# A fused attention-and-SoLU kernel whose written-out order of all steps is made anew

## The chip, the cores and the metric

The kernel runs on one core of a Trainium2 chip. The metric is the time of one execution on the device in microseconds (us); of several executions the median counts. A core has five engines with an instruction queue each: TensorE (PE, products; its weight loads are shown as PEld), VectorE (DVE), ScalarE (ACT), GpSimd (POOL) and SyncE (SP, which here issues all transfers between HBM and the core's memory). Each engine works through its own queue in order, and the engines wait for one another by semaphores.

## The reference

Two softmax reads between 512 tokens and 32 states, for 8 batches and 8 heads, give 544 rows per batch; those rows go through a feed-forward layer with the SoLU activation and a layer norm.

```python
# x: (8, 8, 512, 64)   state: (8, 8, 32, 64)   scale = 1/8
a      = softmax(scale * x @ state.T)        # over the 32 states
xread  = a @ state                           # 512 token rows
a2     = softmax(scale * state @ x.T)        # over the 512 tokens
sread  = a2 @ x                              # 32 state rows
rows   = concatenate([xread, sread], axis=2) # heads side by side: (8 * 544, 512)
h      = rows @ w_in                         # (4352, 1024)
solu   = h * softmax(h)
ln     = (solu - mean) / sqrt(var + 1e-6) * g_ln
out    = ln @ w_out                          # (4352, 512)
```

The activations are float32. The weights w_in and w_out arrive as 64-bit floats and are turned to float32 on the chip.

## The kernel before, in words

**Tiles.** The 4352 rows are 34 tiles of 128 rows: tiles 0 to 31 hold the token rows (tile t belongs to batch t // 4), tiles 32 and 33 hold the state rows of all batches. For the token rows the kernel never forms `xread`: it first multiplies state and w_in for each batch (a 256 x 1024 matrix per batch, "state_w_in"), and then h = a @ state_w_in.

**Steps.** The work is cut into named steps, each a Python generator; one step of the order runs a generator to its next `yield`. The names that the tables use are these:

- `l n`, `cl n`, `c n`: the load of one 512 KB piece of the weights (n 0 to 7 is w_in, row block n // 2 and column half n % 2; n 8 to 15 is w_out), and its conversion to float32: ScalarE takes the low words (L232), VectorE makes two bit operations (L243, L246), and VectorE or GpSimd the addition (L249).
- `Ls`, `G`: load and copy of the states; `LT b i`, `Ln b i`: loads of x in two layouts.
- `V b n`: column half n of state_w_in of batch b: 8 products on TensorE (L199; the trace has 16 records for them) and two evictions on ScalarE (L142). For batches 0 and 1 the result stays on the core (`swf`, its PSUM bank is called `swph`); for batches 2 to 7 it goes to HBM and is read back later (`Y`, `Z`, tiles `vt`, `kept`, `swf`; PSUM `swps`).
- `S b`: scores of batch b (TensorE, L199, tiles `sps`); `E b`: softmax over tokens; `A b` or, for batch 0 in two halves, `Ah 0 k`: softmax over states, which ends in `aT` (tiles 4b and 4b+1 of batch 0 need the first half, the other two the second); `R b`: the state rows (L421, L432).
- `P b j`, `wo n`, `wi c`: split of a float32 matrix into a high and a low part. A product of two split matrices is made as three products (high x high, low x high, high x low). Batch 0 and the output products of tiles 0 and 1 use plain float32 instead.
- `wg f`: rows of w_out scaled by -g (tile `wog`), on ScalarE (L267) or VectorE (L269).
- `H t`: h of tile t on TensorE (L473) into one of two pairs of PSUM banks; `C t`: maximum (L480), exponential (L483), product (L486), centring (L491 on ScalarE or L493 on VectorE), sum of squares (L498) and a root on GpSimd (L500 to L503); `D t`: a 32 x 32 block transpose on VectorE (L510) and a round trip through HBM (tiles `ub`, `ut`, `back`) that completes the transpose; `T t`: high part `uh` (L142 on ScalarE, L144 on VectorE) and low part `ul` (L147); `O t`: output products (L541 plain, L547 split), eviction (L554, L556) and store (L560).
- `K`: one product of two 128 x 128 identity tiles into a bank that nobody reads (L571, tile `warm`; the trace has two records for each).

**What sets the order.** The text `ORDER` lists all steps in one line of issue, `name*count` for several in a row. `issue` walks through it, so each engine's queue is that list with the other engines' instructions left out; nothing reorders it later. The string table `OPT` says which engine does a step with a choice (a, d, p for ScalarE, VectorE, GpSimd), and `PLACES` gives each tile its place in the core's memory or its PSUM bank. A tile that is put on a place waits until the last reader of the tile that was there is done. `T t` needs `D t`, which needs most of `C t`, which needs all of `H t`; TensorE fills that chain's time with products of other tiles, as the order says.

Of the kernel before, what the change touches and what calls it, by code (L numbers as in the profile page):

```python
# [39 lines left out]
V10 c7 K LT00 V20 c3*2 c5*2 cl7 K cl5 c5 LT01 S0 c7 cl12 Ah01 E0 Lg K*6 E0*5 Ah00 V10*2 Ah00*2 l1 cl1 Ah00 K Ah01*3 K  # L40
c1 K*2 Ls2 G2 K V30 l8 l10 K*2 V30 K*2 l9 l11 K V30 K*2 G2 V40*2 Lg LT10 K*2 Ah00 c8 V40 V50*2 c9 V50 c1*2 V01 Ah01
l13 Ah00 c8 Ah00 Lg c13 V51*2 V11 V51 E0*2 Lg cl8 V31 Ah00 l14 c13 Ah00 K l15 Y51 V31 c14*2 Lg V01*2 V31 cl14 c14 K c8
Ah01 cl13 V11 Ah01 K E0 c15 Ah01 V70 wg0 V70*2 Y30 H0*2 V11 P10 C0 Ah01 cl10 C0 P11 wg6 c10 V21 c10 V21*2 H1 Ln01 c12
Ln11 K*2 C0*2 c10 H1 Ln00 C1*2 V41 E0 C0 V71*2 V41*2 LT31 V71 H2*2 P11 Y31 c12 cl9 D0 C1 D0 C1 c15 V60*2 c11 V60 C1
c9*2 R0 wg1 D1 R0*3 C2 P10 R0 wo4 R0 LT11 S1 Z51 D1 H3 V61 H3 E1*4 D0 A1*2 wg4 c11 Y41 c13 wg5 cl11 c11 D1 C2*2 A1 Y40
A1 C3 T0 O0 wg2 wg3 T0 O0*4 C2 D2 C3 C0 Y50 O0*2 V61*2 LT41 T1 O1*4 T1 O1 cl15 c15 A1 wg7 E1 wo7 D2 C2 E1 C1 C3*2 D3
Y20 O0 A1*2 C2 O1*3 A1*3 Z31 D3 D2 H4 O1 LT21 C3 E1*2 A1 H5 wo5*2 wo4 H4*5 H5*2 D3 T3 H5*3 wo7 LT20 Y60 S2 E1 C4*2 C3
O3*2 C4 T3 O3 T3 O3 Ln10 Y61 O0*2 E2 T2 O3*2 E2 C4 wo6 E2*2 Z20 H6 O3*2 P31 T2 O2*2 C5 H6*2 Y71 D4*2 O1 O2*2 wo6 C5
O3*2 A2*2 C5 A2*2 C5 H7 D5 C5 A2 H6*3 O2 H7 T3 O3*2 O2 O3 T2 O2 T2 E1 C6 A2*2 P20*2 D4 C4*2 T4 O2*4 LT30 D5 H7*2 C6
O2*2 O4 R1*2 T4*2 O4 Y21 C6 O4*3 Z50 R1 A2 S3 D5 C6 E2 O4*2 A2*2 T4 Z21 D6*2 E3 O3 A3*2 A2 E2 Z30 E2 Y70 T5 O4 T5 O4  # L50
P21*2 H7*2 C7 H8*2 O5 D6 O5 O4 E2 E3 C7 O4*3 O5*2 T5 LT40 C7*2 T5 A3 T6 D7 O5*2 C6 H8*4 O5 D7 P31 O5*3 C8*2 E3 O2 E3*3
# [24 lines left out]
H32 C31*2 H32*2 C31 H32 D31 D30 D31 H32*3 wi2 H32*2 O28*3 H32 O28 H32*2 H33*2 O29*3 O25 O29*3 T30 T29 H33 O29 T30*2
O29*3 C32*3 D31 T31 C32 D32*2 C30 O29*2 H33*3 O29*2 O30 C30 T31 H33 T31*2 H33*5 O30*8 O31 C31 O31*5 C33*4 D33 C33 D32
T32*4 C33 O31*2 O28 O31*2 C31 O32*2 O31 O30 O31 T30 O30*3 D33*2 O30 T33 O32*6 O31*2 O33*4 T33 O32 C32 O32 O33 T33
O33*5 T33 O33 O32 C32 O32 O33*10 O32 O33 O32 O33*6
"""  # L80

# [6 lines left out]
    sm='0123103210321032103210321031023102',  # L88
# [567 lines left out]
```

## Time and profile before

| what | value |
|---|---|
| executions | 363.46, 363.64 and 366.76 us, median 363.64 us |
| the profiled execution | 366.5 us, span from first to last instruction 364.6 us |
| TensorE busy | 346.6 us (95% of the span) |
| VectorE busy | 282.6 us (77%) |
| ScalarE busy | 216.2 us (59%) |
| GpSimd busy | 190.2 us (52%) |
| DMA, main queue | 91.77 MB, 71.9% of 16 engines' span |
| granted TensorE clock | 1.000 |

A busy time is the time in which at least one instruction of that engine ran. In a list of groups, the columns are line, engine, operation, tiles, shapes and count, then busy time, mean duration of one in ns, and the idle time just before with what ended it. In a timeline the columns are start, duration from the first start to the last end of the merged run, engine, line, operation, tiles, shapes and count, and in brackets the idle time before it and what ended it. Products overlap in TensorE, so a row's duration is a little more than the distance to the next row's start.

### The profile page before, as it was taken

Reading aid. Unit: us, or ns where it says so; the run is one execution under the profiler, and the core shown is the slowest. Engines: PE = TensorE matmul, PEld = TensorE weight load, DVE = VectorE, ACT = ScalarE, POOL = GpSimd, SP = SyncE. Lnnn points to the kernel's source line nnn. Section 1 sums busy time; section 2 is a strip of 40 time slices with the busy share of each in tenths; the row PEclk is TensorE's granted clock in tenths of the full one; section 3 lists DMA queues with packets and bytes.
Section 4 is the critical chain, followed back from the end, with each engine's and each line's share of the span. In section 5 each row is a group of like instructions: output and inputs, shape, how many; then the busy total and the mean of one; then the engine's idle time right before and its main releaser. Section 6 shows DMA issues by size and latency. Waiting matters only on the chain.

```text
span 364.6 us, 6200 instructions
## 1 busy us (share of the span) xinstructions
PE 346.6 (95%) x2274; PEld 255.5 (70%) x2274; DVE 282.6 (77%) x393; ACT 216.2 (59%) x350; POOL 190.2 (52%) x245
## 2 busy tenths in 40 slices
PE   5399999999899999999999999999999999999996
PEld 4153333468677787868888677887888888888885
DVE  4679999979797878977988999889649767866500
ACT  3277998877657973848564765646367456324421
POOL 2131275646669564345959253538677743740280
PEclk9999999999999999999999999999999999999999
DMA  7995999999889999667796797585756145344442
GB/s 253 398 400 210 347 317 335 332 343 351 290 243 341 351 323 326 211 212 257 243 363 224 261 293 287 177 293 223 262 176 222 76 166 187 125 143 152 180 146 74
DMA packets 47086, 92.16 MB, mean 253 GB/s; under 512 B 4176, under 2 KB 25936, under 8 KB 47056
## 3 DMA queue, kind: packets, MB, share of 16 engines
q1 hardware_dynamic: 47056, 91.77, 71.9%
q8 instruction: 18, 0.29, 0.3%
q14 instruction: 12, 0.10, 0.1%
HBM read 54.53 MB, written 37.22 MB: 252 GB/s over the span
## 4 chain that ended last, share of the span: by engine, by line
PE 62%; DMA 14%; DVE 12%; issue 4%; ACT 4%; SPq 2%; POOL 1%; ACTq 0%; DVEq 0%; POOLq 0%
PE o L547 34%; PE h L473 20%; DMA back<-ut 6%; DMA ut<-ub 3%; DMA st<-stB_dram 3%; DMA kept<-vt 2%; PE swps L199 2%; PE swph L199 2%; DVE ub L510 2%; PE srps L421 2%; DVE sm L480 2%; PE sps L199 2%; DVE u L486 1%; ACT e L483 1%; DVE swl L147 1%
## 5 line engine op out<-in xcount | busy, mean ns | idle before, releaser
L147 POOL TENSOR_TENSOR ul<-back,uh 128x512 fp32r<-128x512 f32 x46 | 61.1, 1335 | 48.7 <-DVE uh L144 25.3
L547 PE MATMUL o<-wohi,uh 128*128 128x512 f32 (+1 forms) x264 | 70.6, 386 | 2.0 <-ACT uh L142 1.6
L547 PE MATMUL o<-wohi,ul 128*128 128x512 f32 (+1 forms) x264 | 71.3, 384 | 0.4 <-POOL ul L147 0.4
L547 PE MATMUL o<-wolo,uh 128*128 128x512 f32 (+1 forms) x264 | 71.3, 385 | 0.0
L483 ACT ACTIVATE e<-h,sm 128x1024 f32<-128x1024 f32 x34 | 37.9, 1114 | 39.3 <-DVE sm L480 36.0
L547 PEld LDWEIGHTS o<-wohi,uh 128*128 128x128 f32 x264 | 48.2, 188 | 13.7 <-ACT uh L142 2.4
L486 DVE SCALAR_TENSOR_TENSOR u<-h,e 128x1024 f32<-128x1024 f32 x34 | 41.4, 1218 | 20.7 <-ACT e L483 20.4
L547 PEld LDWEIGHTS o<-wohi,ul 128*128 128x128 f32 x264 | 48.7, 188 | 11.4 <-POOL ul L147 0.8
L547 PEld LDWEIGHTS o<-wolo,uh 128*128 128x128 f32 x264 | 48.3, 188 | 11.2 <-issue 1.7
L480 DVE TENSOR_REDUCE sm<-h 128x1 f32<-128x1024 f32 x34 | 41.2, 1213 | 14.0 <-PE h L473 8.2
L510 DVE STREAM_TRANSPOSE ub<-u 128x1024 f32<-128x1024 f32 x34 | 42.0, 1236 | 5.6 <-ACT u L491 5.0
L142 ACT ACTIVATE uh<-back 128x512 fp32r<-128x512 f32 (+1 forms) x46 | 28.2, 624 | 27.3 <-DMA back<-ut 27.3
L498 ACT ACTIVATE e<-u 128x1024 f32<-128x1024 f32 x34 | 35.8, 1052 | 5.6 <-DVE u L493 5.3
L554 ACT ACTIVATE osb<-o,sm 128x512 f32<-128x512 f32 (+1 forms) x29 | 19.2, 666 | 26.7 <-PE o L547 6.6
L473 PE MATMUL h<-swh,ath 128*128 128x512 f32 x112 | 35.0, 398 | 0.0
L473 PE MATMUL h<-swl,ath 128*128 128x512 f32 x112 | 34.5, 391 | 0.0
L473 PE MATMUL h<-swh,atl 128*128 128x512 f32 x112 | 34.4, 389 | 0.0
L491 ACT ACTIVATE u<-u,sm 128x1024 f32<-128x1024 f32 x20 | 23.0, 1150 | 13.5 <-DVE u L486 13.5
L147 POOL TENSOR_TENSOR swl<-swf,swh 128x1024 fp32r<-128x1024 f32 x11 | 26.4, 2399 | 2.9 <-ACT swh L142 1.7
L249 POOL TENSOR_TENSOR wf<-wf,r 128x512 uint32<-128x512 uint32 x9 | 11.8, 1310 | 27.7 <-DVE wf L246 11.4
L473 PEld LDWEIGHTS h<-swh,ath 128*128 128x128 f32 x112 | 20.6, 188 | 5.9 <-issue 1.7
L473 PEld LDWEIGHTS h<-swh,atl 128*128 128x128 f32 x112 | 21.0, 188 | 4.5
(87 smaller groups left out, 533.8 us busy)
## 6 DMA issues: line engine op xcount, KB each, us to landing
ut<-ub SPq DMA_DIRECT2D x34, 512.0 KB, 3.5
back<-ut SPq DMA_DIRECT2D x34, 512.0 KB, 4.5
out_dram<-osb SPq DMA_DIRECT2D x33, 256.0 KB, 3.8
xT<-xT_dram SPq DMA_DIRECT2D x16, 512.0 KB, 7.9
xn<-xn_dram SPq DMA_DIRECT2D x16, 512.0 KB, 6.4
kept<-vt SPq DMA_DIRECT2D x12, 512.0 KB, 6.6
swf<-kept SPq DMA_DIRECT2D x12, 512.0 KB, 6.3
raw<-w_in_dram SPq DMA_DIRECT2D x8, 512.0 KB, 8.5
```

The source lines that it names most:

```text
L142: nc.scalar.activation(out, src, AF.Copy)
L147: engine(k).tensor_tensor(out=out, in0=a, in1=hi.bitcast(F32), op=ALU.subtract)
L199: nc.tensor.matmul(banks[j][at:at + NS, :], state_of(b, head), moving(head // 2)[h * D:(h + 1) * D], start=True, stop=True)
L473: nc.tensor.matmul(ph[t][:, cols], left[l][:, p, tok], weights[:, cols], start=(p, l, r) == (0, 0, 0), stop=(p, l, r) == (parts - 1, *kind ...
L480: nc.vector.tensor_reduce(nm, ph[t], AX.X, ALU.max, negate=True)
L483: nc.scalar.activation(e, ph[t], AF.Exp, bias=nm, accum_out=z)
L486: nc.vector.scalar_tensor_tensor(out=u, in0=ph[t], scalar=1.0, in1=e, op0=ALU.mult, op1=ALU.mult, accum_out=su)
L491: nc.scalar.activation(u, u, AF.Identity, bias=su, scale=-float(DF))
L498: nc.scalar.activation(e, u, AF.Square, scale=float(DF) ** -0.5, accum_out=ss)
L510: nc.vector.transpose(ub, us[t][0])
L547: nc.tensor.matmul(po, ut[t][l][:, f, :], w[NP + f // 2][:, f % 2, cols], start=(hf, l, w is wohi, q) == (0, 0, True, 0), stop=(hf, l, q) ...
L554: nc.scalar.activation(o[:, cols], po, AF.Copy, scale=us[t][1])
```

## The change

The tables `ORDER`, `OPT` and `PLACES` are replaced; no function is changed, and the same products, conversions and transfers are made. One line is added to a table, so every line number after it is one higher. `ORDER` holds 27 `K` steps instead of 37. `OPT` moves some steps between engines: counted over the whole kernel, of the 64 low parts `ul` VectorE makes 25 instead of 18 and GpSimd 39 instead of 46; ScalarE makes 49 instead of 46 of the 68 high parts `uh`, 7 instead of 4 of the 8 scalings of w_out, and 30 instead of 27 full-width evictions of output tiles; VectorE makes 3 instead of 6 of those.

```diff
-OPT = dict(ph=2, k4=45, direct=[0, 1], hn=[0], vh=[0, 1], ah=[0], on=[0, 1], s2='pppp', add='ddddppdddppppppp',
-           whi='aaaa', wlo='ddpp', wg='daaaddda', woh='aaaa', wol='dppd', ev='aaaaaaaaaaaaaaaaaaaaaaaaaaaaaaaa',
+OPT = dict(ph=2, k4=45, direct=[0, 1], hn=[0], vh=[0, 1], ah=[0], on=[0, 1], s2='pppp', add='dpdpdddpppppppdd',
+           whi='daad', wlo='ddpd', wg='aadaaaaa', woh='adaa', wol='dppd', ev='aaaaaaaaaaaaaaaaaaaaaaaaaaaaaaaa',
...
 ORDER = """
-l0 cl0 l4 c0*3 c4 cl4 c4*2 l2 K c2 K*5 c2 l12 c12 K l6 c6*2 K*3 cl2 c2 cl6 c6 l3 c3 cl3 Ls0 G0*2 V00*3 l5 l7 c7 V20*2
+l0 c0*2 l2 c2 cl2 c2*2 Ls0 G0*2 K*4 cl0 c0 l6 cl6 l4 K*4 c6 c4 cl4 c4 c6 c4 l5 c6 c5*2 V30 cl5 K LT00 V30 c5 V30 l3
...
```

**SyncE, the start of the program.** The first loads are, before (`raw n` is the piece of weights of `l n`, `st` the states of four batches, `xT0` the x of batch 0):

```order
L220 DMA raw0_86<-w_in_dram 128x1024
L220 DMA raw4_90<-w_in_dram 128x1024
L220 DMA raw2_102<-w_in_dram 128x1024
L223 DMA raw12_114<-w_out_dram 128x1x1024
L220 DMA raw6_119<-w_in_dram 128x1024
L220 DMA raw3_133<-w_in_dram 128x1024
L176 DMA st0_138<-stB_dram 128x1024
L220 DMA raw5_156<-w_in_dram 128x1024
L220 DMA raw7_158<-w_in_dram 128x1024
L204 DMA xT0_0_187<-xT_dram 128x1024
L204 DMA xT0_1_200<-xT_dram 128x1024
```

and now:

```order
L221 DMA raw0_86<-w_in_dram 128x1024
L221 DMA raw2_91<-w_in_dram 128x1024
L177 DMA st0_99<-stB_dram 128x1024
L221 DMA raw6_112<-w_in_dram 128x1024
L221 DMA raw4_116<-w_in_dram 128x1024
L221 DMA raw5_131<-w_in_dram 128x1024
L205 DMA xT0_0_151<-xT_dram 128x1024
L221 DMA raw3_156<-w_in_dram 128x1024
L205 DMA xT0_1_160<-xT_dram 128x1024
L177 DMA st2_200<-stB_dram 128x1024
L221 DMA raw7_205<-w_in_dram 128x1024
```

The states move from seventh to third place, the second half of x of batch 0 from eleventh to ninth, and the piece of w_out that stood fourth to a later place. The four even pieces of w_in (0, 2, 4, 6), which the first column halves of state_w_in need, are complete at place five, as before.

**TensorE, the first product tiles.** Around the first two `H` steps there stands, before (`h0` is H of tile 0, `swps2` and `swps4` are `V 2 1` and `V 4 1`):

```order
L473 MATMUL h0_438<-swf0_0_143,aT0_0_388 128x512 x2
L473 MATMUL h0_438<-swf0_1_144,aT0_0_388 128x512 x2
L199 MATMUL swps2_0_1_460<-wf0_92,s2_0_140 32x512 x2
L199 MATMUL swps2_0_1_460<-wf1_106,s2_0_140 32x512 x2
L199 MATMUL swps2_1_1_461<-wf2_96,s2_0_140 32x512 x2
L199 MATMUL swps2_1_1_461<-wf3_121,s2_0_140 32x512 x2
L473 MATMUL h1_473<-swf0_0_143,aT0_0_388 128x512 x2
L571 MATMUL warm_104<-ident_74 128x128 x2
L473 MATMUL h1_473<-swf0_1_144,aT0_0_388 128x512 x2
```

and now (`sps1` is the scores of batch 1, `swps5` is `V 5 1`):

```order
L474 MATMUL h1_439<-swf0_0_258,aT0_0_349 128x512 x2
L474 MATMUL h1_439<-swf0_1_259,aT0_0_349 128x512 x2
L572 MATMUL warm_104<-ident_74 128x128
L200 MATMUL sps1_0_464<-xT1_0_374,s2_0_101 32x512 x4
L200 MATMUL sps1_1_465<-xT1_1_330,s2_0_101 32x512 x4
L474 MATMUL h0_486<-swf0_0_258,aT0_0_349 128x512 x2
L474 MATMUL h0_486<-swf0_1_259,aT0_0_349 128x512 x2
L572 MATMUL warm_104<-ident_74 128x128 x4
L200 MATMUL swps5_0_1_527<-wf0_88,s2_2_202 32x512 x2
```

Tile 1 goes ahead of tile 0, and the scores of batch 1 stand between them instead of after tile 2. Ahead of this place stand 14 of the 18 `V` and `S` steps that precede the first output product, where before there were 12. Of the 37 `K` steps before, 10 stood ahead of the first `V`, 25 from there to the first `H` and 2 after it; now 8, 8 and 11. All stand ahead of the first output product, before and now.

**ScalarE, ahead of the first output products.** The instructions around the first `uh` (high part, or plain copy for tiles 0 and 1) are, before:

```order
L142 ACTIVATE uh0_678<-back0_650 128x512
L267 ACTIVATE wog5_682<-wf5_458,ngT_82 128x512 x2
L142 ACTIVATE uh0_678<-back0_650 128x512
L491 ACTIVATE u2_669<-u2_669,sm2_605 128x1024
L483 ACTIVATE e3_693,sm3_676<-h3_629,sm3_676 128x1024
```

and now:

```order
L268 ACTIVATE wog4_633<-wf4_256,ngT_82 128x512
L143 ACTIVATE uh1_639<-back1_551 128x512
L233 ACTIVATE r11_661<-raw11_220 128x512
L268 ACTIVATE wog4_633<-wf4_256,ngT_82 128x512
L484 ACTIVATE e3_669,sm3_601<-h3_553,sm3_601 128x1024
L143 ACTIVATE uh1_639<-back1_551 128x512
L268 ACTIVATE wog5_556<-wf5_328,ngT_82 128x512
```

More scalings of w_out (`wog`) stand on ScalarE, close ahead of the products that read them, and the exponential of tile 3 stands between the two halves of the first `uh`.

More of the change, by code (lines that the diff above doesn't have):

```diff
@@ new lines @@
+T2 O3*2 E2 O3*2 Z21 O2 C5*2 O3*2 O2*3 A2*2 E2 Z61 T2 H6 O3*2 LT30 H6 D5*2 C7 R0 T4 C2 E2 R1*2 O2 H6*4 P20 C7 O2 E2
+O2*3 C7 R0 O0 C7 A2 C7 R1 Z41 O4*2 A2*2 R1 H9 O2 P21 O4*2 R1*2 P20 H9 T4 O4 T4 O4*3 C4 C6 A2 C6*2 T4 C6 D7 S3 E3 D6 C6
+O4*5 H9*2 P21 H9*2 C6 E3*4 D5 T5*2 E3 C5 H8 E3 H8 Y51 O5*3 H8 T5 H8*2 D7 D6 T5 O5 C9 O5*2 C9 E3 O5 C9 O5*5 O2 C9 D9 R0
+O5 Z31 P31 D7 D6 T7*2 H11*2 A3 T6 H8 C8 LT41 A3 H11 O7 A3 O7 C8 O7 C8 C9 D9 A3 C8 P31 T6 O7*3 O6*4 H10 P61 H10*2 O6*2
+T6 Z30 P30 O6 E2 T6 H10*3 P30 T7 O6 A3 O6*2 O4 O5 O6 D9 T9 Ln21 O6*2 D8 O7 LT40 C8 C9 A3*2 D8 O9 E2 Ln20 D8 C7 O9 O6
@@ new lines @@
+H11 O7*2 T7 O7*2 P61 O7 T9*2 C10 O9 H11 Ln31 O9*2 H11 O9*2 C10*3 E3 A3*2 D10 S4 A4 D10 O7 T8 Ln30 R2*3 O9*2 A3 C8
+C11*2 O8 T8 O8*5 H12 C10 C11*2 H12 A3 H12 H13 E3 H13 H12*2 A4 T8 O8*2 E4 T9 O8*2 T8 E4*2 C11 D10 Ln61 O8*2 A4*2 O7 O8
+H12 R3 T10 R3 Z40 R2 D11 E4*3 C12 H13 A4*3 D11 O10 C12 O10 LT50 T10 C12 O10*2 C10 R3 P40 O10 R2 H13 O9 H13*2 E4*2 LT51
+E4 D11 R2 O9*3 wi1 H14*3 O8 T10*2 O10*2 C13 C12 D12*2 C13*2 H14*3 S5 E5 P41 C13*2 R3*2 A4 R3 O10*4 T11 O11*2 O10*2
+T11*2 E4 O11*2 E5 O11*2 T11 D13 O11*2 D12 O9 A4 C14 D13 A5*3 H15*3 O11*3 A4*2 C14 H15 E5 C12 E5 C11 LT61 O11 T12*2
@@ new lines @@
+O12*4 C14 T12 O11 Ln41 O12*2 C14 H15 C14 T12 P40 D13 Ln40 H15 C15 LT60 D14 O12*3 P41 C15 H16 O12*3 O11 H16*2 T13*2 O10
+C15*2 T13 C14 H16*2 O13*3 H16 E5*2 H17*4 D15 Z50 D14 D15 Ln51 D14 R4*2 A5 C12 O12 S6 R4*2 C16 O13*2 D15 O13*5 C15 C16
+E6*2 R4 LT71 C16*3 E5*2 A5 T14 T13 O13*2 D16*2 H18*2 R4 A5 E5 A5 A6 C16 H17 O12 H18*2 C13 H18 O14 T14*3 D16 O13 H17
+T15 C17*2 T15*2 H18 O14 A6 O14*3 LT70 A6 O13 C17*3 O15*2 T15 O15*3 O14*2 Z51 Ln60 O14*4 O15*3 D17*2 P50*2 E6*2 E5
+O14*2 O15*2 H19 T16 H19*3 E6 O15 C18 E6 T16 E6 O16 P51 O16 C18 A5*2 Ln50 C15 O15*2 O16*2 T16 O16 H19 D17 H19 O16 C18
@@ new lines @@
+O26*2 O25*2 H29 O25 C26 O25*2 T25 C28*3 D28 C28 O26 wi0 O25*2 T27 O25*2 O27 O25 wi2 O27 C27 T27*2 H29*3 C29*4 O25
+H30*3 wi3 O27 H30*3 O26 O27*7 T27 O27*2 O26 D29 D28*2 H31 T28 wi2 O27 wi3 H31*3 O26 C30*2 D29 R7 X O26*2 H31 O26 T28
+C26 O28 H31 C30 O28 O26 X H32 O28 C30 D29 T29 C31*2 D30*2 O27 T28*2 H32*5 C31*3 O28*6 H32*2 D31 H33*2 C31 O26 O28*2
+H33 D31 H33 D31 H33*2 O28*2 H32*4 C32 T31*2 H33*4 T31 C32 H33 T31 H33 O31*13 C32*2 O29*2 D32 O29*2 D30 T29*2 D32*2 T29
+O29 T30*2 O29 C33 O29 O30*3 C33*2 O29*3 C33 D33*2 O28 O29*2 D33 O30 T32 O32 C29*2 O30 O32*3 T32 O32 T32*2 O32*2 O30
@@ L80 @@
+O32*2 T30*2 O30*2 O31 O30 O32 O29*2 T33*2 C32 T33*2 O30*2 O32 O30 C30*2 O30 O33 O30 O33*4 C33*2 O33*11 C32 O32*3
+O33*12
 """
 PLACES = dict(
[L84 to L87 removed]
@@ L94, in issue @@
+    sm='0123012301321032103210321031201323',
+    o='0100100101011010110101000101010101',
+    t='01231231231231231231231321321313213103231320213200302301123102113012330301231230132102301230',
+    h='01010101011101011010101010100101010101')
 def issue(nc, steps, order):
```

83 lines of the change are left out of this document (29 added, 54 removed).

## The prediction

> **What bounds the kernel now.** I read the page of the profile first, then a table by stage, then TensorE's timeline of the first 76 us. The page:
>
> ```profile
> span 364.6 us, 6200 instructions
> ...
> PE 346.6 (95%) x2274; PEld 255.5 (70%) x2274; DVE 282.6 (77%) x393; ACT 216.2 (59%) x350; POOL 190.2 (52%) x245
> ...
> PE 62%; DMA 14%; DVE 12%; issue 4%; ACT 4%; SPq 2%; POOL 1%; ACTq 0%; DVEq 0%; POOLq 0%
> ```
>
> TensorE is busy for 95% of the span and carries most of the chain that ended last. The table by stage cuts the span at the first useful product (14.64), the first product of an H step (36.97), the first output product (60.60) and the last product; its columns are the stretch, its length, and the busy time of TensorE, its weight loads, VectorE, ScalarE and GpSimd, the clock, the share of the DMA engines and GB/s:
>
> ```profile
> 0.00:14.64 14.64, 4.64 (x21) 4.35 (x21) 7.78 (x13) 4.63 (x6) 2.59 (x9) 1.00 0.86 307
> 14.64:36.97 22.33, 21.54 (x242) 10.05 (x243) 17.56 (x36) 14.53 (x29) 4.56 (x7) 1.00 0.85 323
> 36.97:60.60 23.63, 23.13 (x213) 8.96 (x206) 22.21 (x37) 21.24 (x37) 12.40 (x9) 1.00 0.96 321
> 60.60:361.10 300.50, 297.31 (x1809) 232.17 (x1807) 235.00 (x310) 175.37 (x279) 170.65 (x221) 1.00 0.70 242
> 361.10:364.60 3.50, 0.00 (x0) 0.00 (x0) 0.00 (x0) 0.43 (x1) 0.00 (x0) 1.00 0.21 75
> ```
>
> From 60.60 on, TensorE waits for only 300.50 - 297.31 = 3.2 us in 300. That stretch holds the same products after the change, so an order can save there 3.2 us at most. The rest is the opening: 60.6 us until the first output product, in which TensorE looks busy but in part with warm-up products. Its timeline there:
>
> ```profile
> 1.34 4.64 PE L571 MATMUL warm<-ident 128*128 128x128 f32 x20 [1.34 <-POOL ident masks.py:199]
> 14.64 2.62 PE L199 MATMUL swph<-wf,s 64*32 64x512 f32 x16 [8.66 <-POOL s L144]
> 16.34 2.62 PE L199 MATMUL swps<-wf,s 64*32 64x512 f32 x16
> ...
> 20.61 0.71 PE L571 MATMUL warm<-ident 128*128 128x128 f32 x4
> 21.25 1.09 PE L199 MATMUL sps<-xT,s 64*32 64x512 f32 x16
> 22.27 2.72 PE L571 MATMUL warm<-ident 128*128 128x128 f32 x22
> ...
> 31.45 1.09 PE L199 MATMUL swph<-wf,s 64*32 64x512 f32 x16 [0.79 <-DVE wf L249]
> ...
> 36.97 3.70 PE L473 MATMUL h<-swf,aT 128*128 128x512 f32 x8
> 40.60 1.09 PE L199 MATMUL swps<-wf,s 64*32 64x512 f32 x16
> ...
> 52.23 1.10 PE L421 MATMUL srps<-xn,e 128*32 128x64 f32 x64
> 53.83 0.45 PE L432 MATMUL srT<-ident,sr 128*64 128x64 f32 x8 [0.50 <-DVE sr L425]
> ...
> 60.59 13.90 PE L541 MATMUL o<-wog,uh 128*128 128x512 f32 x32
> ```
>
> TensorE waits 8.66 us for the copied states; the scores of batch 0 start at 21.25 and the first H at 36.97, 15.7 us later, with warm-up products in between. What feeds this opening is the load queue. The landings show in who waited for them: first, second, seventh and ninth transfer.
>
> ```profile
> 4.71 0.67 ACT L232 ACTIVATE r<-raw 128x512 uint32<-128x512 uint32 x1 [2.71 <-DMA raw<-w_in_dram]
> 5.95 0.67 ACT L232 ACTIVATE r<-raw 128x512 uint32<-128x512 uint32 x1 [0.57 <-DMA raw<-w_in_dram]
> ...
> 13.98 1.27 POOL L144 COPY s<-st 64x512 f32<-64x512 f32 x2 [4.79 <-DMA st<-stB_dram]
> ...
> 16.52 0.43 DVE L243 TENSOR_SCALAR wf<-raw 128x512 uint32<-128x512 uint32 x1 [2.80 <-DMA raw<-w_in_dram]
> ```
>
> All these transfers are 512 KB, and they land one after the other: (16.52 - 4.71) / 8 = 1.48 us apart on average. So a load's place in SyncE's queue gives its landing time, before and after.
>
> **The change part by part.**
>
> *States third.* They land near 8 us instead of 13.9, so the 8.66 us wait breaks up. But the first V step also needs the fourth and fifth transfer and their conversions on VectorE, so it ends near 15 instead of 17 us. What counts is the next step. The scores of batch 0 need both halves of x, now at places seven and nine instead of ten and eleven; the ninth landed at 16.5. The scores therefore start near 16.1 instead of 21.25.
>
> *From the scores to the first H.* Lower bound: the same 15.7 us as before, which puts the H step of tile 1 at 31.8. Upper bound: no gain, 36.97 (all that follows hangs on another engine). In between lies ScalarE, whose prices are:
>
> ```profile
> 23.76 0.69 ACT L355 ACTIVATE e2T<-sps,sc 128x512 f32<-128x512 f32 x1 [1.98 <-POOL sc L351]
> ...
> 29.45 0.63 ACT L386 ACTIVATE a<-a 128x512 f32<-128x512 f32 x1
> ...
> 49.21 2.05 ACT L142 ACTIVATE vt<-swps 128x512 f32<-128x512 f32 x4
> ```
>
> In the new order ScalarE's queue holds, from the first exponential of the scores to the last eviction that this H needs, 20 evictions at 0.51 (2.05 for four), 2 conversions at 0.67, and 2 + 2 exponentials, at 0.9 with their sums read and at 0.63: 10.2 + 1.3 + 1.8 + 1.3 = 14.6 us. The first exponential came 2.5 us after the scores began (23.76 - 21.25), so now near 18.6, and the H of tile 1 can start at 33.2 if ScalarE never waits. I take 33.7, near this row, since the wait for the states of the other batches (tenth place, near 18) lies beside it. That is 3.3 us earlier than 36.97, with two more V or S steps behind it.
>
> *From the first H to the first output product.* TensorE's queue has four H steps at 3.63 (40.60 - 36.97), three V, one S and the sums of R at 1.1, and 11 warm-up products, which are 22 records, 2.7 us as in the row at 22.27: 14.5 + 5.5 + 2.7 = 22.7 us. For waits I put the 0.79 + 0.50 = 1.3 us that TensorE had between 14.64 and 60.59. The first output product then comes at 33.7 + 22.7 + 1.3 = 57.7 instead of 60.6: **-2.9 us**. Bounds: no wait and H at 31.8 give 54.5 (-6.1); VectorE and ScalarE, both over 90% busy in this stretch before, give back all of it (0). The ten dropped warm-up products lie within this term, and are no gain of their own: where TensorE would stand idle anyway they cost nothing.
>
> *A store on SyncE.* The turned softmax of batch 0 now goes out at place 21, ahead of half of the x of batch 1, a piece of w_out and the loads of g, which all wait until VectorE has made it. Before, it stood behind all loads. The 20 loads ahead of it land until about 4.7 + 19 x 1.48 = 32.8, and VectorE makes it as its 32nd instruction, 13 ahead of the first half of `aT` that H needs at 33.7, and so some 6 us earlier: the load queue hides the wait. If it came 3 us after 32.8, g and the scalings of w_out would come as much later, and the first output product with them.
>
> *The turning of R of batch 0* (0.45 us) moves behind the first output product: **+0.45**. The part of it that was a wait is counted above.
>
> *Engines chosen anew.* Seven more low parts on VectorE and seven fewer on GpSimd, three more high parts and more scalings on ScalarE. From 60.6 on these engines are busy for 235, 171 and 175 of 300 us, so this load lies beside TensorE's work as long as each tile's chain ends in time. The waits of TensorE there were 3.2 us; I take 3.5 (**+0.3**), with none and three times as much as the ends.
>
> *The end.* The last tile is again tile 33 in two halves, and 3.5 us follow the last product as before: nothing.
>
> Sum: -2.9 + 0.45 + 0.3 = -2.15, about -2.2. The span becomes 362.4. The profiled execution took 366.5, 1.9 more than its span, so it becomes 364.3; it lies 2.9 above the median of the runs, and a stretch that is the same in each run moves all of them alike: 363.64 - 2.2 = **361.4 us**.
>
> **A rule weighed: the first products.** A warm-up record took 4.64 / 20 = 0.23 us at 1.34 and 2.72 / 22 = 0.12 at 22.27; the V steps at 14.64 and 16.34 lie 1.70 us apart, while such a group takes 1.09 from 21.25 on. TensorE thus needs its longer times for 4.3 to 6.6 us after useful work began (to 18.96 at least, to 21.25 at most). In the new order TensorE has 18.6 us with little work ahead of the scores, and fewer warm-up products. The Trainium skill, page "TensorE: Matmul & The Clock Gate", Part 1, says that the array runs at half rate after an idle window of about 3.4 us and at full rate after about as long of sustained work. By that rule the products behind the scores make themselves fast by about 20 us; the sum is unchanged unless gaps keep the array at half rate, which is a rival below. The trace agrees in kind; its 4.3 to 6.6 us are longer than the rule's 3.4.
>
> **The rivals.**
>
> *A, faster by over 1%.* TensorE does not wait at all until the first output product (-1.3), and half of its 3.2 us of waits later go (-1.9 against the 3.5 assumed): 361.4 - 3.2 = 358.2. For it: the steps are written so that every chain has cover. Against it: 3.2 us in 300 is already little, and a new order has its own misses.
>
> *B, no gain.* VectorE sets the pace. It was busy 22.21 of 23.63 us from the first H to the first output product, and the new order puts no less ahead of the first four block transposes on it: counted in its queue, 65, 76, 87 and 91 instructions instead of 63, 69, 84 and 87. If it idles in the opening as before (22.33 - 17.56 = 4.8 us), the first output product comes no earlier: 363.6.
>
> *C, slower: chains longer than their cover.* A tile's chain, from the last product of H to the first `uh`, costs by these rows (page, groups and DMA issues):
>
> ```profile
> L483 ACT ACTIVATE e<-h,sm 128x1024 f32<-128x1024 f32 x34 | 37.9, 1114 | 39.3 <-DVE sm L480 36.0
> ...
> L486 DVE SCALAR_TENSOR_TENSOR u<-h,e 128x1024 f32<-128x1024 f32 x34 | 41.4, 1218 | 20.7 <-ACT e L483 20.4
> ...
> L480 DVE TENSOR_REDUCE sm<-h 128x1 f32<-128x1024 f32 x34 | 41.2, 1213 | 14.0 <-PE h L473 8.2
> L510 DVE STREAM_TRANSPOSE ub<-u 128x1024 f32<-128x1024 f32 x34 | 42.0, 1236 | 5.6 <-ACT u L491 5.0
> L142 ACT ACTIVATE uh<-back 128x512 fp32r<-128x512 f32 (+1 forms) x46 | 28.2, 624 | 27.3 <-DMA back<-ut 27.3
> ...
> L491 ACT ACTIVATE u<-u,sm 128x1024 f32<-128x1024 f32 x20 | 23.0, 1150 | 13.5 <-DVE u L486 13.5
> ...
> ut<-ub SPq DMA_DIRECT2D x34, 512.0 KB, 3.5
> back<-ut SPq DMA_DIRECT2D x34, 512.0 KB, 4.5
> ```
>
> That is 1.21 + 1.11 + 1.22 + 1.15 + 1.24 + 3.5 + 4.5 + 0.62 = 14.5 us when nothing queues. The cover is the TensorE work that stands between in the order. From the chain that ended last, the price of a split product and what the two transfers cost where they met others:
>
> ```profile
> 85.91 4.12 DMA ut<-ub
> 90.08 6.94 DMA back<-ut
> ...
> 280.76 9.52 PE o L547 x42
> ```
>
> At 0.227 us a product (9.52 / 42) the smallest covers are now 17.4, 17.2 and 17.4 us for tiles 22, 24 and 27, and 15.9 and 15.4 for tiles 31 and 32; before they were 17.5, 16.2, 17.2 and 14.1 for tiles 24, 25, 28 and 33. With transfers of 11.1 us as above a chain takes 17.6, and any queueing on an engine is then a wait. It decides when the chains of 22, 24 and 27 take over about 20 us: three waits of 3 us make +9 on the forecast, 370.4. Against it: the covers before were no larger and TensorE hardly waited.
>
> *D, slower: TensorE keeps its longer times in the opening.* If gaps keep it at the 1.70 us of the first groups, the 13 V and S groups from 16.1 on take 1.70 each and the 7 warm-up products among them 0.46, together 25.3, and H starts at 41.4 instead of 33.7: +7.7, 369.1. It decides when such groups still take that long past about 30 us.
>
> **How the numbers follow.** The forecast has 0.43, A 0.25, B 0.15, C 0.12, D 0.05. A measurement of this kernel tells about 1% (3.6 us) from no change. Faster by over 1%, below 360.0: A and 0.05 of the forecast's own spread, 0.30. Slower by over 1%: C and D, 0.17. Within 1%: the rest, 0.53. The range leaves out the far part of A and most of C: 357.4 to 367.4.
>
> **What would show it.** In the changed profile: the scores of batch 0 near 16 us and the first H near 33.7; the first output product near 57.7; TensorE idle for about 3.5 us from there to the last product. B shows as an H step that is earlier but an output product that is not; C as rows of TensorE that wait for `uh` or `ul` beyond 4 us in all; D as V steps still 1.7 us apart after 25 us. The prediction is wrong if the opening is not shorter, or if the long stretch loses more than the opening gains.

## The result, and the profile after

The changed kernel takes 361.58 us (median of 14 runs, 359.52 to 363.06), the kernel before 364.87 (median of 14, 363.31 to 366.76): a ratio of 0.9906, 95% interval 0.9882 to 0.9930. The forecast was 361.4. The profiled execution took 360.81 us, its span is 358.7. The two profiled executions lie 5.7 us apart and the medians 3.3, because the one of before was among its longest and the one of after among its shorter ones; so the times below rest on medians, and the traces of several kernels are read beside each other where a place is named.

The page of the changed kernel:

```profile
span 358.7 us, 6148 instructions
PE 345.6 (96%) x2254; PEld 253.8 (71%) x2254; DVE 280.5 (78%) x392; ACT 218.5 (61%) x357; POOL 186.0 (52%) x239
PE 71%; DMA 13%; DVE 7%; issue 4%; ACT 2%; SPq 2%; POOL 1%; ACTq 0%; POOLq 0%; DVEq 0%
```

TensorE now carries 71% of the chain that ended last instead of 62%, VectorE 7% instead of 12%. The table by stage, cut at the first useful product, the first H, the first output product and the end of the last (columns as before: stretch, length, busy TensorE, weight loads, VectorE, ScalarE, GpSimd, clock, DMA share, GB/s):

```profile
0.00:9.24 9.24, 3.78 (x16) 3.49 (x16) 3.54 (x6) 2.51 (x3) 1.89 (x8) 1.00 0.75 250
9.24:34.94 25.70, 23.57 (x240) 7.12 (x241) 21.53 (x41) 17.71 (x35) 6.32 (x8) 1.00 1.01 381
34.94:58.96 24.02, 23.18 (x182) 10.63 (x183) 23.57 (x37) 21.22 (x37) 11.37 (x14) 1.00 0.74 247
58.96:355.10 296.14, 295.10 (x1818) 232.54 (x1816) 231.85 (x310) 176.88 (x284) 166.43 (x210) 1.00 0.72 249
355.10:358.70 3.60, 0.00 (x0) 0.00 (x0) 0.00 (x0) 0.19 (x1) 0.00 (x0) 1.00 0.31 109
```

The first output product comes at 58.96 instead of 60.60, 1.6 us earlier, where 2.9 were forecast. The long stretch is 296.1 instead of 300.5 us: 4.4 shorter, where it was forecast 0.75 longer. TensorE's timeline of the opening:

```profile
9.24 2.60 PE L200 MATMUL swps<-wf,s 64*32 64x512 f32 x8 [4.11 <-POOL s L145]
13.34 2.52 PE L200 MATMUL swps<-wf,s 64*32 64x512 f32 x8 [1.50 <-DVE wf L250]
...
16.51 2.11 PE L200 MATMUL sps<-xT,s 64*32 64x512 f32 x16
...
34.94 3.67 PE L474 MATMUL h<-swf,aT 128*128 128x512 f32 x8
...
47.39 1.98 PE L474 MATMUL h<-swf,aT 128*128 128x512 f32 x4 [0.84 <-DVE aT L398]
...
58.96 2.74 PE L542 MATMUL o<-wog,uh 128*128 128x512 f32 x6
```

The wait of 8.66 us for the states has become two, 4.11 and 1.50, and the scores start at 16.51 instead of 21.25. But the first H starts only 2.0 us earlier (34.94 against 36.97). What TensorE waited for behind the first output product, before and after (engine and line, whom it waited for: us in total, times, longest):

```profile
PE o L547 <- ACT uh L142: 1.6, 2, 1.0
PE srps L421 <- ACT osb L554: 0.6, 1, 0.6
PE o L547 <- POOL ul L147: 0.4, 1, 0.4
PE o L547 <- DVE uh L144: 0.4, 1, 0.4
```

```profile
PE sps L200 <- DMA xT<-xT_dram: 0.6, 1, 0.6
```

The list holds idle times over 0.15 us. Before, output products waited for `uh` and `ul`, the last steps of a tile's chain; after, no product of the whole stretch does.

### The profile page after: what moved, and what is told of

Same layout as the page of the kernel before. It is cut to its first block, busy times and chain, and to the rows that moved or that the text cites. A ratio compares the mean times of both kernels' runs of the same rounds, so it can differ in the third digit from the quotient of the medians.

```text
span 358.7 us, 6148 instructions
## 1 busy us (share of the span) xinstructions
PE 345.6 (96%) x2254; PEld 253.8 (71%) x2254; DVE 280.5 (78%) x392; ACT 218.5 (61%) x357; POOL 186.0 (52%) x239
## 4 chain that ended last, share of the span: by engine, by line
PE 71%; DMA 13%; DVE 7%; issue 4%; ACT 2%; SPq 2%; POOL 1%; ACTq 0%; POOLq 0%; DVEq 0%
PE o L548 40%; PE h L474 21%; PE o L542 3%; DMA back<-ut 2%; DMA xT<-xT_dram 2%; DMA raw<-w_in_dram 2%; PE sps L200 2%; DMA ut<-ub 2%; PE srps L422 2%; DVE sm L481 1%; DVE u L487 1%; DMA raw<-w_out_dram 1%; PE swps L200 1%; DMA xn<-xn_dram 1%; DMA out_dram<-osb 1%
## 5 line engine op out<-in xcount | busy, mean ns | idle before, releaser
L148 POOL TENSOR_TENSOR ul<-back,uh 128x512 fp32r<-128x512 f32 x39 | 52.7, 1360 | 69.0 <-DVE uh L145 29.8
L555 ACT ACTIVATE osb<-o,sm 128x512 f32<-128x512 f32 (+1 forms) x32 | 21.4, 672 | 42.6 <-PE o L548 20.8
L499 ACT ACTIVATE e<-u 128x1024 f32<-128x1024 f32 x34 | 35.8, 1054 | 12.3 <-DVE u L494 12.2
L143 ACT ACTIVATE uh<-back 128x512 fp32r<-128x512 f32 (+1 forms) x49 | 29.9, 622 | 17.3 <-DMA back<-ut 17.1
L474 PE MATMUL h<-swh,ath 128*128 128x512 f32 x112 | 36.5, 407 | 0.1
L148 POOL TENSOR_TENSOR swl<-swf,swh 128x1024 fp32r<-128x1024 f32 x12 | 31.0, 2584 | 3.7 <-issue 2.2
L200 PE MATMUL swps<-wf,s 64*32 64x512 f32 x192 | 19.4, 636 | 6.2 <-POOL s L145 4.1
L250 POOL TENSOR_TENSOR wf<-wf,r 128x512 uint32<-128x512 uint32 x9 | 12.9, 1438 | 22.7 <-DVE wf L247 17.2
```

The lines of the kernel that those rows point to most:

```text
L143: nc.scalar.activation(out, src, AF.Copy)
L148: engine(k).tensor_tensor(out=out, in0=a, in1=hi.bitcast(F32), op=ALU.subtract)
L200: nc.tensor.matmul(banks[j][at:at + NS, :], state_of(b, head), moving(head // 2)[h * D:(h + 1) * D], start=True, stop=True)
L474: nc.tensor.matmul(ph[t][:, cols], left[l][:, p, tok], weights[:, cols], start=(p, l, r) == (0, 0, 0), stop=(p, l, r) == (parts - 1, *kind ...
L499: nc.scalar.activation(e, u, AF.Square, scale=float(DF) ** -0.5, accum_out=ss)
L555: nc.scalar.activation(o[:, cols], po, AF.Copy, scale=us[t][1])
```

## The experiments

Two theories stood against each other at first: the prediction's (the opening gives the gain, the rest gives a little back), and one read from the two traces (the order behind the first output product gives most of it). The other parts (slots, engine strings, warm-up products, load places) were changed one at a time.

### Slots made anew, in both kernels

Only the strings of places change: each buffer takes the slot whose last reader stands furthest back in the order. The cut shows the string of the large buffers; those of the output rows (`o`) and of PSUM banks (`t`) are made anew as well.

```diff
 # kernel before
-    k4='0123456789ABCDEFGHIJKLMNOPQRSTUVWXYZabcdefghi0148BAFEKLQPNTOefcdMR6USgJVcTd...
+    k4='0123456789ABCDEFGHIJKLMNOPQRSTUVWXYZabcdefghi0148BAFEKLQPNTOcfdeRMU6gAJSPdT...
 # changed kernel
-    k4='0123456789ABCDEFGHIJKLMNOPQRSTUVWXYZabcdefghi204569DCEKPHLSFXgbQ6i4eM5GTPSg...
+    k4='0123456789ABCDEFGHIJKLMNOPQRSTUVWXYZabcdefghi240659CEDKPHLFSXQgb05ie6MGQTBR...
```

> The kernel before, order and engines untouched; only the slot strings (blocks, output rows, banks) are written anew, so that each buffer takes the slot whose last reader stands furthest back. In the kernel before 9 of 349 reused slots are written again less than 20 issued instructions after their last reader; with the new strings none. If slots written too soon make TensorE's later waits (3.2 us from the first output product on), they fall to about 1 us and the time to about 362.8 from 364.9. If not (my theory: the slots cost nothing), 364.9 +- 0.8.

> The changed kernel with slot strings made by the same rule (the slot whose last reader is furthest back), nothing else. It is the yardstick for the two mixed kernels, whose slots are made by that rule too. All theories: 361.6 +- 0.8; first output product near 59.0, waits of TensorE behind it near 1 us.

Measured: 365.93 us for the kernel before (1.0029 of its own time, 1.0007 to 1.0051) and 364.72 for the changed one (0.9985 of the kernel before, 0.9959 to 1.0010). Both expectations failed, the first narrowly: its range without an effect was 364.9 +- 0.8. Before did not get faster, and from its first output product on TensorE was idle for 3.0 us again (261.39 - 258.38), so these slots took no wait away; whether they put new ones in place of old ones was not tested. The changed kernel lost 3.1 us, nearly all of its gain. Its trace shows where: what VectorE waited for from 60 to 72 us, and what TensorE waited for behind the first output product:

```profile
DVE u L484 <- DMA kept<-vt: 3.7, 1, 3.7
```

```profile
PE h L471 <- DVE u L484: 1.9, 1, 1.9
PE sps L197 <- DMA xT<-xT_dram: 0.5, 1, 0.5
PE o L545 <- ACT osb L552: 0.4, 1, 0.4
```

The new `u` had been put into the slot of a `vt` whose store still stood in SyncE's queue. VectorE, which works in order, stood still for 3.7 us, the PSUM half that this step frees came free late, and TensorE waited 1.9 us. A third version makes only the string of the large buffers anew, and counts a buffer that a store reads last as taken for 100 more issued instructions:

> The changed kernel; only its block slots are made anew, by the rule of after_own_slots with one thing added: a buffer whose last reader is a store on SyncE's queue counts as free only 100 issued instructions later (there 9 of 51 such buffers were written again within 60 instructions, here none within 100). after_own_slots took 364.7 against 361.6, and VectorE waited there 3.74 us for the store of a `vt` whose slot the next `u` had taken. If such waits for stores are what foreign slots cost, the time comes back to 361.6 +- 0.8 and that wait is gone. If the slots cost in another way (banks, other readers), it stays near 364.7.

Measured: 361.58 us (0.9906 of the kernel before, 0.9870 to 0.9941), the changed kernel's own time, and TensorE's waits behind the first output product are one of 1.0 us, for x. So new slots for the large buffers cost nothing when those under a store are left alone, and the waits for a store, 1.9 us on TensorE, are the largest part of the 3.1 us. The rest is not separated: the third version has the `o` and `t` of the changed kernel, the second has its own.

### The two halves of the order, exchanged

The step list of one kernel up to its first output product, then the remaining steps in the order of the other, with slots by the first rule. Each step keeps the engine of the kernel that its place comes from, so order and engines go together here. Around the joint of the first (old steps are those from `Y51` on):

```diff
 c9 cl11 wg1 H2*2 C3 c11 K T1 K A1 K
-O1*3 wg3 S2 A1 C2*2 P10 Z20 C3*2 O1*2 C2 H7*2 ...
+Y51 Y30 Ln11 LT31 P11 C0 R0 P10 R0 wo4 R0 Z51 Y41 wg5 C3 C2 O1 wg3 O1*4 ...
```

> The order of the changed kernel up to its first output product, then all remaining steps in the order of the kernel before (tiles 0 and 1, and 2 and 3, change names there, since the new opening begins with tile 1; each step keeps the engines of the kernel its place comes from). If the prediction's split is right (the opening gives -2.9, the rest +0.3), the time is about 362.0 or below, against 364.9 before. If the gain is half from the order behind the first output product, as the two traces suggest (opening 60.6 to 59.0, -1.6; the rest about -1.7 of the 3.3 between the medians), about 363.3, with some 3 us of waits behind the first output product. If the opening gives nothing at the end, 364.9.

> The other way round: the order of the kernel before up to its first output product (with its 37 warm-up products), then the remaining steps in the changed order. If the prediction's split is right, about 365.2 (the old opening, and +0.3). If half of the gain is from the rest, about 363.2: first output product near 60.6, waits behind it near 1 us. If all of it is from the rest, 361.6.

Measured: 376.89 us (1.0342, 1.0296 to 1.0387) and 373.27 us (1.0225, 1.0185 to 1.0265): both far slower than either kernel, so the time as a whole decides nothing between the theories. TensorE's waits from 60 to 100 us, in the kernel with the new opening and in the one with the new rest:

```profile
PE o L531 <- ACT wog L257: 4.4, 1, 4.4
PE o L537 <- ACT uh L132: 3.1, 1, 3.1
```

```profile
PE sps L190 <- DMA xT<-xT_dram: 7.9, 1, 7.9
PE o L532 <- DVE wog L260: 1.7, 1, 1.7
```

At the joint the scalings of w_out and the loads of x of batch 2 are where the other half does not want them. Behind it the mixed kernels can be compared with their parents. All orders end with the same work: the last 1600 products hold 1032 split products of H and O in each (340 and 692, or 336 and 696, at the same price) and the same 48 half-width ones, scores, and products of R. Their stretch, in the kernel before and in the mixed kernel that ends in its order:

```profile
60.59:100.08 39.49, 38.51 (x210) 25.09 (x208) 34.62 (x44) 30.32 (x47) 23.88 (x34) 1.00 0.94 337
100.08:361.02 260.94, 258.81 (x1601) 207.09 (x1599) 200.39 (x269) 145.01 (x231) 146.78 (x188) 1.00 0.66 227
```

```profile
109.45:371.19 261.74, 258.76 (x1601) 206.89 (x1599) 204.06 (x269) 145.15 (x231) 146.90 (x190) 1.00 0.64 224
```

and in the changed kernel and the mixed kernel that ends in the new order:

```profile
58.96:98.39 39.43, 38.80 (x218) 25.44 (x217) 35.81 (x47) 30.52 (x48) 30.20 (x27) 1.00 0.96 346
98.39:354.78 256.39, 256.30 (x1601) 207.10 (x1599) 196.04 (x264) 146.04 (x236) 136.23 (x184) 1.00 0.68 234
```

```profile
111.23:368.58 257.35, 256.83 (x1601) 207.04 (x1599) 196.04 (x263) 146.69 (x236) 136.36 (x184) 1.00 0.66 230
```

The old order takes 260.9 and 261.7 us for them, the new one 256.4 and 257.4, whichever opening stands ahead. Read in the same way from the profiles of the other kernels that keep one order and set of engines:

| | first output product at | from it to the last 1600 products | the last 1600 products |
|---|---|---|---|
| kernel before | 60.6 | 39.5 | 260.9 |
| before_own_slots | 60.5 | 38.1 | 261.4 |
| before_27_warmups | 59.9 | 38.3 | 260.8 |
| changed kernel | 59.0 | 39.4 | 256.4 |
| after_own_slots | 59.9 | 41.7 | 257.1 |
| after_store_slots | 60.1 | 39.7 | 256.5 |
| after_states_sixth | 59.9 | 39.4 | 256.2 |

On the means of three and three, without after_own_slots, whose wait for a store falls into the second column, the opening gives 0.7 us, the next stretch takes 0.9 back, and the last 1600 products give 4.7 (with it 0.6, 1.4 and 4.5). The 0.7 is no more than single executions of one order differ by (59.9 to 60.6, 59.0 to 60.1); the 4.7 is far outside. The gain of the change sits in the last 1600 products, from about 100 us on. The means of three spans differ by 4.1 us, a little more than the medians of the two kernels (3.3).

### The engine strings, exchanged

The order and slots stay, the engine strings are those of the other kernel, with tiles 0 and 1, and 2 and 3, exchanged in the strings by tile. In the changed kernel, in short:

```diff
-add='dpdpdddpppppppdd', whi='daad', ath='aadaaaad', up='aaaddaaaaaadaaddadaaaadddaaaddaddd'
+add='ddddppdddppppppp', whi='aaaa', ath='aaadaaad', up='dadadaaaaaaadadaaaaaadaddadadadddd'
```

> The changed order, slots and places, with the engine strings of the kernel before (tiles 0 and 1, and 2 and 3, exchanged in them, since the new order exchanges their parts). Prediction's term for the engines: +0.3, so without them 361.3 (361 to 362). If the engines make the gain: 364.9. If engines, slots and order only fit as a set, as the slots have shown: slower than 363, with waits of TensorE behind the first output product above 2 us.

> The kernel before with the engine strings of the changed kernel (tiles 0 and 1, and 2 and 3, exchanged). Prediction's term: 365.1. If the engines make the gain: 361.6. If they only fit their own order: slower than 366.

Measured: 398.04 us (1.0889, 1.0831 to 1.0947) and 404.85 (1.1090, 1.1041 to 1.1138): 36 and 40 us more than the same order with its own engines. The largest of TensorE's waits in the changed order with the old engines, over the whole span:

```profile
PE swps L193 <- DVE wf L243: 8.6, 2, 4.5
PE o L541 <- DVE ul L141: 4.8, 4, 1.5
PE o L535 <- DVE z L385: 4.6, 1, 4.6
PE o L541 <- DVE uh L138: 3.5, 3, 2.1
```

The amount of work on each engine differs little between the strings (VectorE 241 of 322 us there, 232 of 296 in the changed kernel behind the first output product). That leaves the place of an instruction in an engine's queue: one that has to wait for an operand holds up all that stands behind it. This is how the waits are read here; the slots, which were written for the other engines, may have a part in them, and no run tells the two apart. A part of the loss is the clock: around some of these waits the granted clock fell to 0.50 (from 70.0 to 76.5 us, for one), and TensorE is busy for 306.0 us behind the first output product, where it is 295.1 in the changed kernel. Neither string is better as such.

### The warm-up products alone

Ten fewer in the kernel before, nothing else (two from the first group, eight from the middle):

```diff
-l2 K c2 K*5 c2 ... cl7 K cl5 c5 LT01 ... E0 Lg K*6 E0*5 ... cl1 Ah00 K Ah01*3
+l2 c2 K*4 c2 ... cl7 cl5 c5 LT01 ... E0 Lg E0*5 ... cl1 Ah00 Ah01*3
```

> The kernel before with 27 instead of 37 warm-up products, nothing else: two less of the ten ahead of the first V step and eight less of the 25 between it and the first H. My theory (they only fill what is idle): 364.8 +- 0.6, first output product at 60.6. If they cost TensorE its time, 10 x 0.24 = 2.4 us less: 362.4. If fewer of them let the clock down, later than 364.8, with V groups 1.70 us apart beyond 21 us.

Measured: 364.63 us, 0.9989 of the kernel before (0.9965 to 1.0014), first output product at 59.93. These ten only filled idle time; the other 27 were kept.

### The load places of the opening

The states back behind the fourth and fifth piece of w_in; and, apart from that, the two halves of x of batch 0 behind three more loads. Every buffer keeps its slot.

```diff
-l2 c2 cl2 c2*2 Ls0 G0*2 K*4 cl0 c0 l6 ... c4 l5 c6 c5*2 V30
+l2 c2 cl2 c2*2 K*4 cl0 c0 l6 ... c4 l5 Ls0 G0*2 c6 c5*2 V30
```

```diff
-cl5 K LT00 V30 c5 V30 l3 c3*2 LT01 S0 ... E0*2 Ls2 G2*2 l7 c7
+cl5 K l3 Ls2 l7 LT00 V30 c5 V30 c3*2 LT01 S0 ... E0*2 G2*2 c7
```

> The changed kernel with the load of the states and its two copies behind the fourth and fifth piece of w_in (sixth instead of third place); every buffer keeps its slot. The states then land near 12.2 instead of 8.0 us and their copies end near 14, but the pieces of w_in land one place (1.3 us) earlier. My theory (x, at places seven and nine, sets the scores): scores near 17, time 361.6 +- 0.8. If the states at place three make the gain of the opening: V and scores about 3 us later, and 1.5 to 3 us at the end.

> The changed kernel with the two halves of x of batch 0 at places ten and eleven, as before, instead of seven and nine (three loads go ahead of them; slots kept). Scores about 19.9 instead of 16.5 to 17.3. If the chain from the scores sets the opening, as the prediction says, H comes 2.7 us later and so does the end: 364.3. If VectorE's work sets it (rival B) and no more than part of the delay lands on VectorE: 361.6 to 362.6.

Measured: 361.27 us with the states sixth (0.9899 of the kernel before, 0.9873 to 0.9925), the same as the changed kernel. Its TensorE:

```profile
13.87 2.98 PE L197 MATMUL swps<-wf,s 64*32 64x512 f32 x16 [8.74 <-POOL s L142]
16.78 0.79 PE L569 MATMUL warm<-ident 128*128 128x128 f32 x2
17.50 1.62 PE L197 MATMUL sps<-xT,s 64*32 64x512 f32 x16
```

The wait of 8.7 us for the states is back, as long as in the kernel before, and costs nothing: with the states at place three TensorE waits twice instead, the second time for a converted piece of w_in, and in both kernels the scores follow straight behind these products and two warm-up records. With x later, 363.27 us (0.9944, 0.9926 to 0.9963): 1.7 more than the changed kernel, or 1.4 by the two ratios. The scores began at 17.27 and not near 19.9, but they stopped for the second half of x:

```profile
17.27 3.30 PE L197 MATMUL sps<-xT,s 64*32 64x512 f32 x16 [0.77 <-DMA xT<-xT_dram]
```

H came at 37.86 and the first output product at 60.80, 2.3 and 1.1 us later than in three kernels with x in its new places (the changed kernel, after_store_slots and after_states_sixth, on the mean 35.6 and 59.7): a part of the delay was taken up on the way. The last 1600 products took 257.1 there. With an opening as long as the old one, the kernel kept more than half of its gain.

### VectorE in the opening

Seven last additions of the conversions to VectorE; in the other kernel three to GpSimd:

```diff
-add='dpdpdddpppppppdd'
+add='dpdpdddddddddddd'   # after_adds_on_vector
+add='dpdpddpppppppppp'   # after_adds_on_gpsimd
```

> The changed kernel with seven last additions of the conversions (pieces 7 to 13) on VectorE instead of GpSimd: 7 x 0.67 = 4.7 us more on VectorE in the opening, 7 x 1.28 = 9 us less on GpSimd. VectorE had 0.4 us of idle time in the 24.0 us between the first H and the first output product. If VectorE sets the pace there, the first output product moves from 59.0 to 62 - 63.7 and the time to 364.6 - 366.3. If not: 361.6 +- 0.8.

> The opposite: the additions of pieces 6, 14 and 15 on GpSimd instead of VectorE, 3 x 0.67 = 2.0 us less on VectorE, 3 x 1.28 = 3.8 us more on GpSimd, which is idle for half of that time. If VectorE sets the pace: 359.6 to 360.6. If what the additions feed then comes later, since GpSimd takes twice as long for one: 361.6 or above.

Measured: 369.13 us (1.0106, 1.0087 to 1.0124) and 363.02 us (0.9933, 0.9916 to 0.9950). The first is slower than any theory had it: the first output product came at 67.0, some 7 us late, for 4.7 us of work. What TensorE waited for longest from 20 to 43 us there, and VectorE from 35 to 43:

```profile
PE swps L193 <- DVE wf L243: 4.1, 1, 4.1
```

```profile
DVE z L383 <- ACT a L380: 2.6, 1, 2.6
DVE wf L243 <- ACT r L226: 2.5, 1, 2.5
```

The additions need ScalarE's rounding, and VectorE, in order, waited for it: a place in a queue adds to the amount of work. And the wait of 4.1 us was followed by slow products: the granted clock was 0.50 from 35.6 to 38.9 us, and four records of a V group took 1.92 us, where 16 take 1.09 elsewhere. The second kernel takes 2.0 us of work off VectorE, and its first output product comes at 59.80, where the mean above has 59.7. So this relief did not shorten the opening, and later a product waited 1.2 us for a low part on GpSimd (`atl`). It does not free VectorE of blame: GpSimd takes 1.28 us for an addition, VectorE 0.67, so what the additions feed comes later as well, and the time is in the range that was expected for that case. Rival B's sum of work alone foretells neither run.

## Why the prediction was right in the sum and wrong in its parts

*The total.* 361.4 forecast, 361.58 measured. That they agree is luck. The change was forecast as -2.2 us and measured as -3.3 (364.87 to 361.58); the forecast counted from the median of three executions, 363.64, which lies 1.2 below the median of fourteen, and this made up for the difference. And -2.2 itself is a sum of two errors: the opening gave less than forecast, the rest gave where it was to take.

*States third, scores near 16.1.* Nearly right: 16.51, though the profiled execution is the earliest; in six other kernels with this opening or with the states sixth the scores start at 17.16 to 17.50. Right too that the states themselves count for nothing and the places of x do: the runs with states sixth and x tenth show it.

*From the scores to the first H: forecast 33.7, measured 34.94, in the variants with slots, states or three additions changed 35.8 to 36.0.* ScalarE's row was priced well: 14.6 us forecast from the first exponential to the last eviction that H needs, 14.99 measured (19.76 to 34.75), and 14.99 or 15.00 in those four variants too. That ScalarE alone is in charge is not shown: in that stretch it is busy for 13.83 us and VectorE for 13.59, and VectorE's `aT` ended at 34.79, the eviction at 34.75. The step that failed is the one ahead of it. The first exponential came 3.25 us behind the scores (3.2 to 3.5 in the variants) instead of 2.5, because the scores themselves were slow:

```profile
16.51 2.11 PE L200 MATMUL sps<-xT,s 64*32 64x512 f32 x16
17.16 1.17 PE L189 MATMUL sps<-xT,s 64*32 64x512 f32 x16
```

The first row is the changed kernel, the second new_opening, which has the same steps up to here. Where the scores took 1.17 us the exponential came 2.73 us behind their start. The 2.5 us were read from the kernel before, whose scores at 21.25 took 1.09; here they come while TensorE still takes its longer times. The prediction had weighed these longer times, up to about 20 us, and left the sum unchanged.

*From the first H to the first output product.* 24.0 forecast (22.7 + 1.3), 24.02 measured.

*The term of the opening.* -2.9 forecast; -1.6 between the two profiled executions, -0.7 between means of three, and on these means nothing is left of it where the last 1600 products begin (98.9 before, 99.2 after).

*The turning of R moved behind (+0.45).* It stands in the 0.9 us that the stretch up to the last 1600 products is longer.

*Engines chosen anew, waits behind the first output product (+0.3).* The failed step, and the larger one: about -4.7 in the last 1600 products. The waits of TensorE there fell from 2.1 us (260.94 - 258.81) to 0.1 (256.39 - 256.30), where they were thought to rise. And the bound that the prediction set, "an order can save there 3.2 us at most", did not hold, since 2.5 us more came out of TensorE's busy time itself, 258.8 against 256.3 us for the same products. Most of this goes with the waits all the same, as the starts of the products in the kernel before show:

```profile
201.12 1.78 PE L199 MATMUL sps<-xT,s 64*32 64x512 f32 x16
...
204.78 0.61 PE L473 MATMUL h<-swl,ath 128*128 128x512 f32 x2
205.24 0.61 PE L547 MATMUL o<-wohi,ul 128*128 128x512 f32 x2
206.25 1.20 PE L547 MATMUL o<-wohi,uh 128*128 128x512 f32 x4 [0.39 <-DVE uh L144]
```

From the start of a row of two products to the next start 0.46 us pass where nothing waits (204.78 to 205.24), and 1.01 where the next product waits for `uh` (205.24 to 206.25); the four behind it take 1.20 us, where four take 1.07 elsewhere. Since products overlap, the row shows 0.39 us of idle time for what cost about 0.7. Four such waits stand in that stretch, 2.1 us of idle time that cost about 3.0. And two of the five groups of scores stretch without any idle time over 0.15 us: 1.78 and 1.45 us, where one takes 1.09 in the changed kernel. TensorE is busy with these 80 records for 6.49 us before and for 5.45 after. Together that is some 4.0 of the 4.5 us; for the rest no place is named. So the step that failed is to take the idle time in the list of waits for all that an order can give. Slots hardly count here: with new ones the stretch took 261.4 and 257.1 us, where each kernel's own gave 260.9 and 256.4. How much is the order and how much the engines stays open, since no run has one without the other that does not wait in many new places.

*Slots.* The prediction gave them no term. In the changed kernel they are worth 3.1 us against a simple rule, most of it ahead of the last 1600 products.

*Warm-up products, no gain of their own; the store on SyncE hidden.* The first is shown by its run. For the second, VectorE's scaling of g ran at 43.69 without a wait for its load; the store was not moved in a run of its own.

*The end, 0.* From the last product's end to the end of the span 3.6 us before (364.6 - 361.02) and 3.9 after (358.7 - 354.78).

*The rivals.* A was right in its later half: the idle time of the long stretch fell from 3.2 to 1.0 us. In its first half it was wrong: TensorE still waited ahead of the first output product, 0.84 us for `aT` at 47.39. B put VectorE in charge from the first H to the first output product. VectorE was busy for 23.57 of the 24.02 us there, but B's sign, an earlier H without an earlier output product, did not show: on the means of three H came 0.8 us earlier and the output product 0.7. C did not happen: no product waited for `uh` or `ul`, with covers of 17.2 us and, near the end, 15.4. D did not happen: V groups of 1.09 us stand from 18.97 on. But the longer times that D is about are what delayed the first exponential.

## What to carry to other kernels

An engine that is 95% busy does not bound what a new order can gain by its idle time: a short wait costs more than the idle time that its row shows, so compare the same set of products in two traces, not only the waits between them. Where queues work in order, the order, the engine of each step and the slot of each buffer are one choice; parts taken from another solution cost 1 to 40 us here, so a planner has to write all three together, and a buffer that a queued store still reads is not free. What a shorter opening gives is not read at its own end: take the difference at a point where both orders have the same work left. And a forecast of a change should be checked against the measured change: here the total was right and the change was not.

## What the runs showed of the hardware

Two things were not expected. First, VectorE's scaling of `u` takes 0.75 us in ten of its 14 places and took 2.68 at 63.38, beside GpSimd's subtractions; its reductions and products beside the same ones kept their 1.19 to 1.21:

```profile
61.01 1.19 DVE L481 TENSOR_REDUCE sm<-h 128x1 f32<-128x1024 f32 x1
62.12 1.21 DVE L487 SCALAR_TENSOR_TENSOR u<-h,e 128x1024 f32<-128x1024 f32 x1
...
63.38 2.68 DVE L494 TENSOR_SCALAR u<-u,sm 128x1024 f32<-128x1024 f32 x1
```

```profile
63.16 2.36 POOL L148 TENSOR_TENSOR atl<-aT,ath 128x1024 fp32r<-128x1024 f32 x1
65.47 2.82 POOL L148 TENSOR_TENSOR swl<-swf,swh 128x1024 fp32r<-128x1024 f32 x1
```

The scaling ends 0.5 us behind the subtraction that began just before it. The Trainium skill, page "SBUF — State Buffer", section "SBUF: two separate sides", says that VectorE, in some of its modes, and GpSimd share a pair of ports as an exclusive lock, which the first holds for its whole instruction while the other is blocked; the trace agrees for this form. Which engine gets a scaling is thus not only a matter of its own queue.

Second, a granted clock of 1.00 does not always show what the first products cost. From the end of the warm-up products on, in the changed kernel and in the one with slots by the simple rule:

```profile
8.60:18.90 10.30, 8.15 (x36) 1.96 (x36) 7.01 (x14) 3.69 (x6) 2.48 (x3) 1.00 1.02 404
```

```profile
8.60:18.90 10.30, 7.44 (x30) 1.66 (x34) 6.25 (x12) 3.68 (x6) 1.94 (x3) 0.50 1.02 410
```

The clock reads 1.00 in the one and 0.50 in the other, but the first eight records of the first V group took 2.60 us in both. The changed kernel's trace holds no record of the clock before 17.81 us, and where none is kept, the column reads 1.00; in the kernel before the first one is at 20.59. The length of the products is the safer sign of the array's rate.
